# Interleaving the first two layer-norm tiles by halves, a shorter root chain, unread products on TensorE, and a convolution branch set back behind its first loads

## The chip, the cores and the metric

One core of one Trainium2 chip. The metric is the device time of one execution in microseconds (us), the median over several executions. "Before" is the kernel without the change, "after" the one with it.

## The reference

A layer norm of `x` feeds two branches whose outputs are added to `x`, and the kernel computes this forward pass together with all gradients for a given `grad_out`. Cut to what matters:

```python
def _fwd_reference(q, k, v, shift_k, ssm_k, ssm_D, x_unused, W_gate, W_up, W_down):
    xn = layernorm(q)                                   # (1, 2048, 1024), bf16
    # branch A: k shifted with 4 taps, times v, long convolution with ssm_k, times xn
    k_shift = sum(k_pad[:, t:t + S] * shift_k[:, 3 - t] for t in range(4))
    kv = k_shift * v
    y = irfft(rfft(kv) * rfft(ssm_k)) + kv * ssm_D
    a = xn * y
    # branch B: gated MLP, F = 3584
    b = (relu(xn @ W_gate) * (xn @ W_up)) @ W_down
    return q + a + b
# outputs: the sum, and its vector-Jacobian product with grad_out for q, k, v,
# shift_k, ssm_k, ssm_D, W_gate, W_up, W_down
```

## The kernel before

The big matrix products of the MLP keep TensorE busy nearly all the time. The convolution branch A is woven between them: both are Python generators that yield an estimate in nanoseconds of the TensorE work just emitted, and a loop takes the next step of branch A whenever the MLP has used up what the branch's last step asked for. So the numbers behind `yield` in the branch decide between which products its steps stand. A scheduler then fixes the order of instructions on each engine at build time, by a model of the machine and by priorities: copies and multiplications of branch A have a `late` priority and go where the model thinks VectorE or ScalarE idle.

The layer norm, one chunk of row tiles after the other (chunks of 1, 1, 2, 2, 2, 4, 4 tiles):

```python
    def layer_norm(self, xn_d, jpool, jtag, spool):
        ...
        for i, n in enumerate(self.LN_CHUNKS):
            ...
            for j in range(n):                                     # row sums on ScalarE
                total = nc.scalar.activation(out=jk[:], in_=xt[:, j, :], func=ACT.Copy, accum_out=sm[:, 0, j:j + 1])
            mean = V.tensor_scalar(out=b(0), in0=f(0), scalar1=1.0 / D, scalar2=None, op0=ALU.mult)
            V.tensor_copy(out=f(1), in_=b(0))
            for j in range(n):                                     # subtract on VectorE, squares on ScalarE
                V.tensor_scalar(out=xt[:, j, :], in0=xt[:, j, :], scalar1=sm[:, 1, j:j + 1], ..., op0=ALU.subtract)
                self.ln_act = nc.scalar.activation(out=jk[:], in_=xt[:, j, :], func=ACT.Square, accum_out=sm[:, 2, j:j + 1])
            ...                                                    # variance, eps, cast: three small operations
            self.ln_act = nc.scalar.activation(out=f(4), in_=f(3), func=ACT.Sqrt)
            V.reciprocal(out=f(5), in_=f(4))
            ...                                                    # five small operations: one Newton step
            self.ln_dve = V.reciprocal(out=self.rstd[:, st0:st0 + n], in_=f(10))
            for j in range(n):                                     # scale, store xn
                V.tensor_scalar(out=xt[:, j, :], in0=xt[:, j, :], scalar1=self.rstd[:, st:st + 1], ..., op0=ALU.mult)
                ...
            yield
```

(Some allocations of tiles and calls that set priorities are left out in these excerpts without a mark.) The MLP's first pass ("flip" transposes a tile of xn on TensorE, and VectorE copies it out of PSUM):

```python
                def gate_up(sp):
                    flip(sp + 2)
                    for s in (sp, sp + 1):
                        ps = self.ps_tile("ps_g")
                        self.gemm8(ps, xT[s], wg)
                        nc.scalar.activation(out=ru[s][:, 0, :], in_=ps[:], func=ACT.Relu)
                        yield 1730
                    for s in (sp, sp + 1):
                        ps = self.ps_tile("ps_u")
                        self.gemm8(ps, xT[s], wu)
                        nc.vector.scalar_tensor_tensor(out=ru[s][:, 1, :], in0=ru[s][:, 0, :], ..., in1=ps[:], ...)
                        ...                                        # ht = product of both, stored by SP
                        yield 1730
                if ahead:                                          # the first block only
                    flip(2)
                    next(ln)
                    yield from gate_up(0)
                    ...
```

The start of branch A, the transposes of its filter (`hn`, 16 of them into one PSUM tile `pst`), and the driver:

```python
    def h_tile(self, st):
        pst = self.ps.tile([P, 16, P], BF16, name="pst", tag="aps")     # pool "aps": two buffers
        for r in range(16):
            self.nc.tensor.transpose(pst[:, r, :], hv[:, r, :], self.identA[:])
        self.vcopy(hT[:, 0:16, :], pst[:])                              # VectorE, late priority

    def steps(self):
        ...
        nx = self.loads_1(0)
        self.loads_2(nx)
        self.pin = False
        hT = self.h_tile(nx)
        for gi in range(self.NG):                                       # eight channel groups
            yield 2000
            yield from self.fwd1_filter(hT, st["sD"], 2000)
            ...
            self.taps(st, ksh, kp, [(3, 0), (2, 1), (1, 2), (0, 3)])    # seven 128x2048 operations on VectorE
            self.tt(kvt[:, 0:16, :], ksh[:], vt[:], ALU.mult)           # and an eighth
            ...
            hT = self.h_tile(nx)                                        # for the next group
            yield 2000
            yield from self.inv_b_chan(Ch, ghn, 2000)                   # products RB x flp, two "aps" tiles
            ...

A_START = 55_000
    ...
    a_steps, left = a.steps(), A_START
    for pace, phase in mlp():
        for ns in phase:
            left -= ns * pace
            while a_steps is not None and left <= 0:
                d = next(a_steps, None)
                ...
                left += d
```

Of the kernel before, what the change touches and what calls it, by code (L numbers as in the profile page):

```python
# [11 lines left out]
BF16 = mybir.dt.bfloat16  # L12
F32 = mybir.dt.float32
I32 = mybir.dt.int32
ALU = mybir.AluOpType
ACT = mybir.ActivationFunctionType
AX = mybir.AxisListType
P = 128
# [24 lines left out]
class ABranch:  # L43
# [381 lines left out]
    def steps(self):  # L425


        self.shift_rows()
        self.pin = True
        nx = self.loads_1(0)  # L430
        self.loads_2(nx)
        self.pin = False
        hT = self.h_tile(nx)
        for gi in range(self.NG):
            st, nx = nx, None
            cg, kp, vt, gt = st["cg"], st["kp"], st["vt"], st["gt"]
            yield 2000
            yield from self.fwd1_filter(hT, st["sD"], 2000)
            Hf = self.flipped
            if gi == 0:  # L440
                self.gate_grad(st)
            ksh = self.lng.tile([P, 16, P], BF16, name="ksh")
            self.taps(st, ksh, kp, [(3, 0), (2, 1), (1, 2), (0, 3)])
            kvt = self.ttile("kvt")
            self.tt(kvt[:, 0:16, :], ksh[:], vt[:], ALU.mult)
            yield from self.fwd1(gt, 2000)
            Gf = self.flipped
            H = self.form("H")
            yield from self.fwd2(Hf, H, 1700)
            if gi + 1 < self.NG:  # L450
                nx = self.loads_1(gi + 1)
            yield from self.fwd1(kvt, 1800)
            Kf = self.flipped
            G = self.form("G")
            yield from self.fwd2(Gf, G, 1700)
            if nx is not None:
                self.gate_grad(nx)
            GKV = self.cmul(H, G, True, "GKV")
            yield 2000
            K = self.form("K")  # L460
            yield from self.fwd2(Kf, K, 1700)
            Y = self.cmul(H, K, False, "Y")
            yield 12000
            yield from self.inv_a(GKV, 1800)
            Cg = self.flipped
            yield 5000
            yield from self.inv_a(Y, 1800)
            Cy = self.flipped
            GH = self.cmul(K, G, True, "GH")
            yield 2000  # L470
            gkv = self.ttile("gkv")
            yield from self.inv_b(Cg, gkv, 2000)
            gks = self.gradients(st, gkv, ksh)
            yield 6000
            yt = self.ttile("yt")
            yield from self.inv_b(Cy, yt, 2000)
            self.store_time(self.y_d, cg, yt)
            yield from self.grad_taps(gi, gks, kp, 1800)
            self.grad_k(st, gks)
            if nx is not None:  # L480
                self.loads_2(nx)
            yield from self.inv_a(GH, 1800)
            Ch = self.flipped
            yield 3000
            if nx is not None:
                hT = self.h_tile(nx)
            yield 2000
            ghn = self.ttile("ghn")
            yield from self.inv_b_chan(Ch, ghn, 2000)
            ghf = ghn[:, 0:16, :].rearrange("p r c -> p (r c)")  # L490
            self.vcopy(self.gD_all[:, gi:gi + 1], ghf[:, 0:1])
            self.store(self.out_gh[cg, :], ghf)
            yield 6000
        self.small_outputs()
# [35 lines left out]
class LnMlp:  # L530
# [52 lines left out]
    def layer_norm(self, xn_d, jpool, jtag, spool):  # L583

        nc, D, V = self.nc, self.D, self.nc.vector

        st0 = 0
        for i, n in enumerate(self.LN_CHUNKS):
            xt = self.ln_x[i]
            self.pri.now()  # L590
            sm = spool.tile([P, 12, 4], F32, name="ln_s")
            smb = spool.tile([P, 4, 4], BF16, name="ln_b")
            f = lambda i: sm[:, i, 0:n]
            b = lambda i: smb[:, i, 0:n]
            for j in range(n):
                jk = jpool.tile([P, D], BF16, name="ln_j", tag=jtag)
                total = nc.scalar.activation(out=jk[:], in_=xt[:, j, :], func=ACT.Copy, accum_out=sm[:, 0, j:j + 1])  # L597
                if i >= 3 and j == 0:
                    self.tc.keep_in_program_order(total)
            mean = V.tensor_scalar(out=b(0), in0=f(0), scalar1=1.0 / D, scalar2=None, op0=ALU.mult)  # L600
            if i == 2:
                self.tc.keep_in_program_order(mean)
            V.tensor_copy(out=f(1), in_=b(0))
            for j in range(n):
                V.tensor_scalar(out=xt[:, j, :], in0=xt[:, j, :], scalar1=sm[:, 1, j:j + 1], scalar2=None,
                                op0=ALU.subtract)
                jk = jpool.tile([P, D], BF16, name="ln_j", tag=jtag)
                self.ln_act = nc.scalar.activation(out=jk[:], in_=xt[:, j, :], func=ACT.Square, accum_out=sm[:, 2, j:j + 1])
            V.tensor_scalar(out=b(1), in0=f(2), scalar1=1.0 / D, scalar2=None, op0=ALU.mult)
            V.tensor_scalar(out=b(2), in0=b(1), scalar1=LN_EPS, scalar2=None, op0=ALU.add)  # L610
            V.tensor_copy(out=f(3), in_=b(2))
            self.ln_act = nc.scalar.activation(out=f(4), in_=f(3), func=ACT.Sqrt)
            V.reciprocal(out=f(5), in_=f(4))
            V.tensor_tensor(out=f(6), in0=f(5), in1=f(5), op=ALU.mult)
            V.tensor_tensor(out=f(7), in0=f(6), in1=f(3), op=ALU.mult)
            V.tensor_scalar(out=f(8), in0=f(7), scalar1=-0.5, scalar2=1.5, op0=ALU.mult, op1=ALU.add)
            V.tensor_tensor(out=f(9), in0=f(5), in1=f(8), op=ALU.mult)
            V.tensor_tensor(out=b(3), in0=f(3), in1=f(9), op=ALU.mult)
            V.tensor_copy(out=f(10), in_=b(3))
            self.ln_dve = V.reciprocal(out=self.rstd[:, st0:st0 + n], in_=f(10))  # L620
            self.pri.now()
            for j in range(n):
                st = st0 + j
                V.tensor_scalar(out=xt[:, j, :], in0=xt[:, j, :], scalar1=self.rstd[:, st:st + 1], scalar2=None,
                                op0=ALU.mult)
                nc.gpsimd.dma_start(out=xn_d[st * P:(st + 1) * P, :], in_=xt[:, j, :])
                self.xn.append(xt[:, j, :])
            st0 += n
            yield
# [34 lines left out]
    def flip_xn(self, st):  # L664
# [4 lines left out]
        self.nc.vector.tensor_copy(out=xT[:], in_=pst[:].rearrange("p a b -> p (a b)"))  # L669
        return xT  # L670

    def hidden(self, first, goT, load, ln, tables, Wg, Wu, Wd, g, xn_d, h_d, ug_d):

        nc, HS = self.nc, self.ST // 2
        for half in range(2):
# [4 lines left out]
            for fb in range(self.FB):  # L680
# [10 lines left out]
                        xT.append(self.flip_xn(len(xT)))  # L691

                def gate_up(sp):
                    flip(sp + 2)
                    for s in (sp, sp + 1):
                        ru[s] = self.e2_tile("ru")
                        ps = self.ps_tile("ps_g")
                        self.gemm8(ps, xT[s], wg)
                        nc.scalar.activation(out=ru[s][:, 0, :], in_=ps[:], func=ACT.Relu)
                        yield 1730  # L700
                        self.pri.now()
# [3 lines that stand above are left out]
                        ht = self.e1_tile("ht")  # L705
                        nc.vector.scalar_tensor_tensor(out=ru[s][:, 1, :], in0=ru[s][:, 0, :], scalar=0.0, in1=ps[:],  # L706
                                                       op0=ALU.is_gt, op1=ALU.mult)
                        nc.vector.tensor_tensor(out=ht[:], in0=ru[s][:, 0, :], in1=ru[s][:, 1, :], op=ALU.mult)
                        stored = nc.sync.dma_start(out=h_d[(s0 + s) * P:(s0 + s + 1) * P, cols], in_=ht[:])
                        self.stored = stored  # L710
                        yield 1730
                        self.pri.now()

                def grad(sp):
                    for s in (sp, sp + 1):
# [9 lines left out]
                        yield 1730  # L725
                        self.pri.now()

                if ahead:
                    flip(2)
                    next(ln)  # L730
                    yield from gate_up(0)
                    next(ln)
                    yield from gate_up(2)
                    next(ln)
                for sp in range(0, HS, 2):
                    self.pri.now()
                    while len(gT) < min(sp + (6 if ahead else 2), HS):
# [4 lines left out]
                    if ahead and sp + 4 < HS:  # L742
                        with self.tc.issue_after(self.stored.ins):
                            load(5 + sp // 2)
                        yield from gate_up(sp + 4)
                        next(ln)
                    if ahead and sp == 0:
                        with self.tc.issue_after(self.stored.ins):
                            first = self.weights(Wg, Wu, Wd, fb + 1)
# [293 lines left out]
```

## Time and profile before

| | before |
|---|---|
| median of the first runs | 1954.47 us (1954.44 to 1956.24, 3 runs) |
| span of the profiled execution | 1957.4 us (its device time, 1959.14, is above those of the timed runs) |
| span of a second profile of the same program, taken later | 1954.3 us (device time 1956.03) |
| TensorE (PE) busy | 98% of the span |
| mean granted TensorE clock | 0.995 (first), 0.996 (second) |
| half-rate stretches of the clock on record (first profile) | from 93.2 us (6.8 us long), 127.3, 400.4 and 704.1 us (3.4 each) |

How to read the lines: "PE pst L293 <- DMA hn: 4.5, 1, 4.5" in the list of waits says that PE waited 4.5 us in total, once, for a load. A line of the timeline gives the start, the length, the engine, the source line, the operation with output, input and shape, the count, and in brackets how long the engine had been idle and what released it. The line numbers of the two kernels differ: L643 of before is L663 of after (the products), L667 is L687 (flips), L706 is L734 (eviction of the up product). `ru` is the tile into which the gate and up products are evicted; `ug_d` and `h_d` are its stores and those of `ht`. The small products of branch A have the operands `RH`, `R`, `FW`, `IA` and `RB`; `flp` is one of the branch's tiles flipped on VectorE, and `B` and `H` are copies out of PSUM made by ScalarE.

### The profile page before, as it was taken

The numbers are of one execution on the slowest core, as the hardware profiler recorded it, in microseconds if no ns is written. First come the engines' busy times: TensorE is split into PE (matmuls) and PEld (weight loads), VectorE is DVE, ScalarE is ACT, GpSimd is POOL, SyncE is SP. The second block draws the span as 40 slices with busy tenths as digits, with TensorE's granted clock in tenths as the row PEclk, the third lists the DMA queues.
The fourth block names the chain that finished last, engine by engine and source line by source line (L and its number), as shares of the span: only waits on it lengthen the run. The fifth ranks groups of instructions, "written<-read, shape, count | busy, mean of one in ns | idle before, by whom it ended". The sixth has DMA issues, their size and how long they took to land.

```text
span 1957.4 us, 36111 instructions
## 1 busy us (share of the span) xinstructions
PE 1915.1 (98%) x15502; PEld 882.0 (45%) x15502; DVE 914.1 (47%) x1374; ACT 616.8 (32%) x852; POOL 14.7 (1%) x37
## 2 busy tenths in 40 slices
PE   7899999999999999999999999999999999999998
PEld 3434444444444444444444444444444444444443
DVE  6677677577678557355255435300222222222222
ACT  6544354444444425444344354311000000000000
POOL 1000000000000000000000000000000000000000
PEclk9999999999999999999999999999999999999999
DMA  9975766984674774462763542691999954545441
GB/s 255 237 157 163 178 179 174 207 202 136 168 193 130 202 213 136 113 185 78 224 158 119 127 135 85 159 324 39 239 255 235 210 135 121 123 120 124 123 121 38
DMA packets 615970, 319.08 MB, mean 163 GB/s; under 512 B 450937, under 2 KB 585089, under 8 KB 615809
## 3 DMA queue, kind: packets, MB, share of 16 engines
q1 hardware_dynamic: 605312, 295.79, 60.2%
q10 hardware_dynamic: 9216, 16.78, 2.8%
q0 software_dynamic: 1280, 4.20, 0.8%
q8 instruction: 121, 1.98, 0.4%
q14 instruction: 41, 0.33, 0.1%
HBM read 141.56 MB, written 95.44 MB: 121 GB/s over the span
## 4 chain that ended last, share of the span: by engine, by line
PE 90%; DVE 4%; DMA 3%; issue 2%; ACT 1%; SPq 0%; POOL 0%; DVEq 0%; ACTq 0%; POOLq 0%
PE ps_w L774 20%; PE ps_x L908 19%; PE ps_o L874 10%; PE ps_g L643 9%; PE ps_u L643 9%; PE ps_d L774 8%; PE ps_h L643 8%; PE ps L66 6%; DMA ln_x<-in_A_q_dram 1%; PE ps_d L794 1%; DVE flp L304 1%; ACT ln_j L597 1%; DMA kp<-in_A_k_dram 1%; DVE gk L74 0%; DVE ru L706 0%
## 5 line engine op out<-in xcount | busy, mean ns | idle before, releaser
L774 PE MATMUL ps_w<-ugs,xn_nat 128*128 128x512 bf16 x1792 | 399.4, 379 | 2.1 <-DMA xn_nat<-xn_d 1.3
L643 PEld LDWEIGHTS <-xnT 128*128 128x128 bf16 x1792 | 172.2, 99 | 218.3 <-issue 19.6
L774 PEld LDWEIGHTS <-xn_nat 128*128 128x128 bf16 x1792 | 170.3, 98 | 208.6 <-issue 5.9
L643 PE MATMUL ps_u<-wu,xnT 128*128 128x512 bf16 x896 | 209.4, 384 | 4.7 <-DMA wu<-in_B_W_up_dram 4.1
L643 PE MATMUL ps_g<-wg,xnT 128*128 128x512 bf16 x896 | 209.0, 383 | 2.2 <-DVE xnT L669 2.2
L643 PE MATMUL ps_h<-wdT,goT 128*128 128x512 bf16 x896 | 206.7, 379 | 0.6 <-DMA wdT<-in_B_W_down_dram 0.6
L921 ACT ACTIVATE w<-xn,m 128x512 f32<-128x512 bf16 x32 | 24.3, 806 | 559.5 <-issue 317.2
L908 PE MATMUL ps_x<-wgT,ggT 128*128 128x512 bf16 x896 | 198.6, 379 | 0.0
L908 PE MATMUL ps_x<-wuT,guT 128*128 128x512 bf16 x896 | 198.6, 379 | 0.0
L874 PE MATMUL ps_o<-wd,hT 128*128 128x512 bf16 x896 | 193.6, 379 | 0.0
L774 PE MATMUL ps_d<-g_nat,hs 128*128 128x512 bf16 x832 | 187.4, 379 | 0.0
L304 DVE STREAM_TRANSPOSE flp<-C 128x1024 f32<-128x1024 f32 x48 | 90.4, 1934 | 102.8 <-ACT C L70 102.8
L829 ACT CAST wi<-ps_w 128x512 bf16<-128x512 f32 x112 | 65.6, 587 | 222.4 <-PE ps_w L774 207.9
L908 PEld LDWEIGHTS <-ggT 128*128 128x128 bf16 x896 | 87.7, 98 | 105.7
L908 PEld LDWEIGHTS <-guT 128*128 128x128 bf16 x896 | 87.7, 98 | 105.7
L874 PEld LDWEIGHTS <-hT 128*128 128x128 bf16 x896 | 87.7, 98 | 105.7
L643 PEld LDWEIGHTS <-goT 128*128 128x128 bf16 x896 | 85.1, 98 | 103.5 <-issue 4.5
L304 DVE STREAM_TRANSPOSE flp<-B 128x1024 f32<-128x1024 f32 x48 | 90.4, 1940 | 83.3 <-ACT B L70 83.2
L910 DVE CUSTOM_DVE_ANT_0 gx<-ps_x,gy 128x512 f32<-128x512 f32 x32 | 22.1, 691 | 216.5 <-PE ps_x L908 216.5
L774 PEld LDWEIGHTS <-hs 128*128 128x128 bf16 x832 | 78.5, 98 | 95.5 <-issue 4.3
L721 ACT CAST gh<-ps_h 128x512 bf16<-128x512 f32 x112 | 65.2, 585 | 165.7 <-PE ps_h L643 153.7
L867 DVE TENSOR_TENSOR ya<-ya,xe 128x1024 bf16<-128x1024 bf16 x16 | 11.1, 692 | 226.9 <-DMA xe<-xn_d 226.9
(165 smaller groups left out, 1541.6 us busy)
## 6 DMA issues: line engine op xcount, KB each, us to landing
ug_d<-ru SPq DMA_DIRECT2D x112, 256.0 KB, 3.5
ugs<-ug_d SPq DMA_DIRECT2D x112, 256.0 KB, 4.6
wg<-in_B_W_gate_dram SPq DMA_DIRECT2D x56, 256.0 KB, 4.2
wu<-in_B_W_up_dram SPq DMA_DIRECT2D x56, 256.0 KB, 3.4
h_d<-ht SPq DMA_DIRECT2D x112, 128.0 KB, 2.4
hs<-h_d SPq DMA_DIRECT2D x56, 256.0 KB, 4.7
out_dram<-wi SPq DMA_DIRECT2D x56, 256.0 KB, 3.1
gt<-in_grad_out_dram SPq DMA_DIRECT2D x32, 256.0 KB, 3.4
```

The costliest lines, as they stand in the source:

```text
L66: self.nc.tensor.matmul(out, lhsT=lhsT, rhs=rhs, start=start, stop=stop)
L304: self.nc.vector.transpose(out=df[:, c0:c0 + 32, :], in_=sf[:, c0:c0 + 32, :])
L597: total = nc.scalar.activation(out=jk[:], in_=xt[:, j, :], func=ACT.Copy, accum_out=sm[:, 0, j:j + 1])
L643: self.nc.tensor.matmul(ps[:], lhsT=xT[:, kt * P:(kt + 1) * P], rhs=w(kt), start=(kt == 0), stop=(kt == self.DT - 1))
L721: nc.scalar.copy(out=gh[:], in_=ps[:])
L774: self.nc.tensor.matmul(ps[:], lhsT=lhsT(st), rhs=rhs(st), start=(st == 0), stop=(st == self.ST - 1))
L794: nc.tensor.matmul(ps[i][:], lhsT=hs(st)[:, j * P:(j + 1) * P], rhs=gn[st][:, ob * 512:ob * 512 + 512], start=(st == 0), stop=(st == self. ...
L829: nc.scalar.copy(out=wo[:, d, :], in_=ps[:])
L874: nc.tensor.matmul(ps[:], lhsT=hT[:, kt, :], rhs=self.wd[:, kt, oc], start=(kt == 0), stop=(kt == self.FT - 1))
L908: nc.tensor.matmul(ps[:], lhsT=T[:, kt, :], rhs=W[:, kt, oc], start=(i == 0), stop=(i == n - 1))
L910: V.tensor_tensor_reduce(out=gx[:, oc], in0=ps[:], in1=gy[:, oc], scale=1.0, scalar=0.0, op0=ALU.add, op1=ALU.add, accum_out=m[:, ob:ob + 1])
L921: nc.scalar.activation(out=w[:, oc], in_=xn[:, oc], func=ACT.Identity, scale=m[:, 5:6], bias=m[:, 4:5])
```

## The change

Its intent is to start TensorE's work earlier: split the first tile's row sums between ScalarE and VectorE, let tile 0 be flipped and multiplied while tile 1 is still normed, cut five operations of the root chain to two, and run 28 products of zeros that nobody reads while TensorE would wait, so that its clock is up when the read ones come. A `yield 8000` stands behind the branch's first loads: these are issued where they were, and all later work of branch A comes 8000 ns (of the estimates behind `yield`) later among the MLP's products. The diff, cut:

```diff
         self.pin = False
+        yield 8000
         hT = self.h_tile(nx)
@@ layer_norm
+            cut = D // 2 if i == 0 else D
+            def row_sums(j, k, func):
+                self.ln_act = nc.scalar.activation(out=jk[:, 0:cut], in_=xt[:, j, 0:cut], func=func, accum_out=sm[:, k, j:j + 1])
+                if cut < D:
+                    if func is ACT.Square:
+                        V.tensor_tensor_reduce(out=jk[:, cut:D], in0=xt[:, j, cut:D], in1=xt[:, j, cut:D], ...)
+                    else:
+                        V.tensor_reduce(out=sm[:, k + 6, 0:1], in_=xt[:, j, cut:D], axis=AX.X, op=ALU.add)
...
-            V.tensor_scalar(out=b(1), in0=f(2), scalar1=1.0 / D, scalar2=None, op0=ALU.mult)
+            yield
+            var = average(2, b(1))
+            if i == 1:
+                self.tc.keep_in_program_order(var)
...
-            V.reciprocal(out=f(5), in_=f(4))
-            V.tensor_tensor(out=f(6), in0=f(5), in1=f(5), op=ALU.mult)
-            V.tensor_tensor(out=f(7), in0=f(6), in1=f(3), op=ALU.mult)
-            V.tensor_scalar(out=f(8), in0=f(7), scalar1=-0.5, scalar2=1.5, op0=ALU.mult, op1=ALU.add)
-            V.tensor_tensor(out=f(9), in0=f(5), in1=f(8), op=ALU.mult)
-            V.tensor_tensor(out=b(3), in0=f(3), in1=f(9), op=ALU.mult)
+            V.reciprocal(out=f(6), in_=f(4))
+            V.scalar_tensor_tensor(out=f(5), in0=f(3), scalar=0.5, in1=f(6), op0=ALU.mult, op1=ALU.mult)
+            V.scalar_tensor_tensor(out=b(3), in0=f(4), scalar=0.5, in1=f(5), op0=ALU.mult, op1=ALU.add)
@@ unread products
+    def warm(self, n):
+        z = self.e1_tile("warm")
+        self.nc.gpsimd.memset(z[:], 0.0)
+        ps = self.ps_tile("ps_warm")
+        for _ in range(n):
+            self.nc.tensor.matmul(ps[:], lhsT=z[:, 0:P], rhs=z[:], start=True, stop=True)
@@ hidden
                 def gate_up(sp):
-                    flip(sp + 2)
                     for s in (sp, sp + 1):
+                        flip(s + 1 if ahead and sp == 0 else sp + 2)
...
+                def chunk():
+                    next(ln)
+                    next(ln)
                 if ahead:
-                    flip(2)
+                    self.warm(28)
+                    chunk()
                     next(ln)
+                    flip(1)
+                    next(ln)
+                    chunk()
                     yield from gate_up(0)
```

## The prediction

> **What bounds the kernel now.** I read the busy times of the page first, then who TensorE (PE) waited for in the first 130 us, the timeline of PE at those waits, and the stretches with their granted clock.
>
> ```profile
> PE 1915.1 (98%) x15502; PEld 882.0 (45%) x15502; DVE 914.1 (47%) x1374; ACT 616.8 (32%) x852; POOL 14.7 (1%) x37
> ```
>
> PE is busy in 1915.1 of 1957.4 us, so all a schedule can win is the other 42 us and whatever PE does slowly. From about 130 us on the list of PE's waits holds only some 10 us, and the last 8 us are the tail after the last product (ends 1949.4). The rest is early:
>
> ```profile
> PE pst_x L667 <- DVE ln_b L609: 10.4, 1, 10.4
> PE pst L293 <- DMA hn<-in_A_ssm_k_dram: 4.5, 1, 4.5
> PE ps_u L643 <- DMA wu<-in_B_W_up_dram: 4.1, 1, 4.1
> PE ps_g L643 <- DVE xnT L669: 2.2, 2, 1.1
> PE pst_x L667 <- DVE ln_x L624: 2.1, 1, 2.1
> ```
>
> The first line is the start: no flip before the first layer norm is done. The second and third are loads that the in-order DMA queue of SP issued late. The timeline of PE at the start:
>
> ```profile
> 10.37 1.03 PE L667 MATMUL pst_x<-ident,ln_x 128*128 128x128 bf16 x8 [10.37 <-DVE ln_b L609]
> 13.45 1.03 PE L667 MATMUL pst_x<-ident,ln_x 128*128 128x128 bf16 x8 [2.05 <-DVE ln_x L624]
> 14.28 5.50 PE L643 MATMUL ps_g<-wg,xnT 128*128 128x512 bf16 x16
> 19.61 3.62 PE L643 MATMUL ps_u<-wu,xnT 128*128 128x512 bf16 x16
> ```
>
> Sixteen products of the same shape take 5.50 us at 14.28 and 3.62 us at 19.61: PE is slow at first. Behind the wait for hn the same is seen, and there the clock is on record:
>
> ```profile
> 94.24 1.92 PE L293 MATMUL pst<-ident,hn 128*128 128x128 bf16 x16 [4.49 <-DMA hn<-in_A_ssm_k_dram]
> 95.95 3.19 PE L643 MATMUL ps_u<-wu,xnT 128*128 128x512 bf16 x7
> 98.94 1.55 PE L66 MATMUL ps<-hT,RH 128*128 128x512 bf16 x4
> ```
> ```profile
> 15.00:16.00 1.00, 1.00 (x4) 0.32 (x3) 0.93 (x5) 0.00 (x0) 0.00 (x0) 1.00 0.19 64
> 97.00:98.00 1.00, 1.00 (x4) 0.29 (x2) 0.42 (x1) 0.00 (x0) 0.00 (x0) 0.50 1.35 164
> 128.00:129.00 1.00, 1.00 (x4) 0.39 (x3) 0.97 (x2) 0.00 (x0) 0.00 (x0) 0.50 0.67 146
> ```
>
> The column before the DMA share is the granted clock: 0.50 at 97 and 128 us, just after the two long waits. At 15 us it says 1.00, yet PE does the same four products in that microsecond; the record of the clock begins with its rise at 18.1 us, so the first slow stretch must be read from the pace.
>
> **What the Trainium skill says.** "TensorE: Matmul & The Clock Gate", section Part 1: The HAM clock gate: the clock starts at half rate, rises after a busy window of about 3.4 us that runs free of the kernel, and falls again after an idle one; 512 columns take 426.7 ns cold, 215.7 warm. The trace agrees: weight loads 0.427 us apart until 18.1, then 16 products in 3.45 net. It adds that 2.3 us of waiting can be enough[...] (half rate at 400 us, after such a wait). "VectorE: DVE Perf Modes", section The perf-mode tier table: tensor_reduce runs at one element per cycle only; this trace has none. The same page, section The TRN2 errata: small operations pay a fixed cost; here a 128x1 VectorE operation takes 0.16 us and the next of a chain starts 0.19 to 0.20 later.
>
> **The change, part by part.**
>
> *Tile 0's norm.* Before: row sum on ScalarE from 3.59 (1.06, plus 0.19 to read the accumulator), usable at 4.77; subtraction 5.15 to 5.63; squares to 6.82; var, eps and cast to 7.38; square root only at 7.76, since tile 1's row sum stands before it; then reciprocal, five small operations, cast, reciprocal, done at 9.78; scaling ends 10.31. After: ScalarE sums 512 columns (estimate 0.53 + 0.19, half of 1.04 plus a fixed part), VectorE the others (estimate 0.65 from 512 cycles). Mean at 4.35, subtraction to 5.2, half squares to 5.98, cast to 6.55. The order of ScalarE still puts tile 1's full row sum (5.87 to 6.83) ahead of the root, so root 6.92 to 7.11. Then reciprocal and two fused operations for reciprocal and five, in all three fewer (0.6 us), but tile 1's mean, cast and subtraction (0.9) lie between. Scaling ends near 9.2: 1.1 us gained.
>
> *Order of flips.* Before, VectorE's queue holds the copy of xnT 0 behind tile 1's whole root chain (flip ends 11.4, copy starts 13.31). After, the copy stands directly behind tile 0's scaling.
>
> *28 unread products.* They start when GpSimd has zeroed their tile, about 1.5 us. They run cold for 3.4 to 6.8 us (where the window lies is chance): 8 to 16 products at 0.427, the rest at 0.216, so they end between 9.2 and 10.9. PE was idle there, but they can hold the flip back by up to 1.7 us. The flip is then warm (16 take 1.06, so 0.53), copy 0.68 + 0.05: first product 10.6 to 12.2 against 14.28.
>
> *Tile 1.* VectorE takes var 1 up only after that copy: three small operations, root, five more, scaling, about 2.45 us: 13.05 to 14.6. Flip 0.53; but tile 2's mean and two subtractions (1.3) stand before the copy, so tile 1's products start 15.1 to 16.6, while tile 0's eight ended 12.3 to 13.9. A new wait of some 2.5 us, partly filled by the flip. Eight gate and sixteen up products at 0.216: end 20.3 to 21.8 against 23.0. Net gain of the start 1.2 to 2.7, less up to 1.6 if the new wait makes the clock fall: I take 1.5.
>
> *The 8000 in the convolution branch.* It moves the transposes of hn behind eight more up and eight down-gradient products (16 x 0.216 = 3.5 us), and the DMA order puts hn one ug store (0.6 us) earlier. hn took 89.19 to 94.24. PE came at 89.75; now it comes 1.5 earlier plus 3.5 later, 91.75; hn's issue moves with the tables, 1.5 + 0.6 earlier, to 87.1, and lands 92.15. Wait 0.4 instead of 4.5. Then no cold stretch: 16 transposes lose 0.6 there, seven up products 1.5, four of RH 0.9, together 3.0. Gain 7.
>
> *The later wu wait.* Before, wu was issued at 122.09 because the ug stores ahead of it waited for two multiplications on VectorE with a 1.9 us flip between (ends 118.98 + 1.93, 120.77 + 0.67). Now the two stand together behind the filter's flips. Counted from the first transposes of hn: PE has 72 products of 512 (15.5) and 5.3 us of branch work before it needs wu, 20.8; flips end 16.1, multiplications 17.5, wu is issued 18.2 and lands 4.4 later, 22.6. Wait 1.8 instead of 4.05, and the 1.7 us lost cold behind it probably too: 3.5 gained.
>
> Sum 1.5 + 7 + 3.5 = 12. The shorter root chains of later chunks hide behind PE.
>
> **Rivals.** (1) The unread products cost what they win: they end late, or zeros don't raise the clock. For: 28 cold ones would last 12 us, to 13.5, and the start would win nothing; total then about 1945. Against: the page speaks of activity, not of values. (2) The waits move instead of going: hn's 4.5 us come back at the filter's flips or at wu, as VectorE and the SP queue stay in order. For: wu is still in the same place behind the stores, and my margin is 2 us. Then only 4 to 6 are won: 1949. (3) Most is luck of interleaving: shifting the branch changes every later meeting of it with the products; the waits after 130 us (10 us, two with a cold stretch of about 1.6) may be won or doubled, 1936 or 1950. (4) The start decides all and the rest follows unchanged: 1.5 to 4 us, 1951.
>
> **Range and chances.** 1954.5 - 12 = 1942.5. Spread: start +-1.5, hn +-2, wu +-3.5, later interleaving +-5; in quadrature 6.6, a little wider upwards: 1935 to 1951. Two per cent are 39 us; PE's own work alone forbids a win that size, and nothing added costs as much.
>
> **What would show it.** The copy of xnT 0 directly behind the scaling near 9.2; first read product at 0.216 pace between 10.6 and 12.2; a wait of about 2 us before tile 1's; end of the first sixteen up products 20 to 22. Hn's wait under 1 us and clock 1.00 from 85 to 105 us; wu's wait under 2.5. Wrong if the unread products still run after 11 us, if the clock falls again before 30 us, or if the sum of PE's waits after 130 us differs by over 5 us.

## The result, and the profile after

After: 1958.3 us median (1955.94 to 1959.82, 4 runs); before, in the same rounds, 1954.45 (1952.49 to 1956.24, 4 runs). The ratio is 1.0019 with a 95% interval of 1.0001 to 1.0036. A ratio here is the mean time of one kernel's fast runs over that of the other's of the same rounds, so not quite the ratio of the medians. Predicted were 1942.5 with a range up to 1951: the change was to win 12 us and lost about 4.

The busy times of the page, and the head of the list of PE's waits, both of after:

```profile
PE 1919.8 (98%) x15530; PEld 884.3 (45%) x15530; DVE 913.0 (47%) x1356; ACT 617.0 (32%) x852; POOL 15.4 (1%) x38
```
```profile
PE ps L66 <- DVE hT L78: 9.7, 4, 2.9
PE ps_g L663 <- DVE ru L734: 3.9, 2, 3.2
PE ps_g L663 <- DVE xnT L689: 3.4, 3, 1.3
...
PE ps L66 <- ACT B L70: 1.6, 2, 1.1
PE ps_warm L698 <- POOL warm L695: 1.5, 1, 1.5
```

The three early waits of before (10.4 us for the first norm, 4.5 for hn, 4.1 for wu) are gone from the list. In their place PE waits more for hT (9.7 us; 6.1 before), and for `ru`, an eviction on VectorE, which was not in the list before.

**The start** went as it was meant to; tile 0's scaling on VectorE ended at 9.21 us (near 9.2 foreseen). The timeline of PE in after:

```profile
1.48 9.14 PE L698 MATMUL ps_warm<-warm 128*128 128x512 bf16 x28 [1.48 <-POOL warm L695]
10.46 0.61 PE L687 MATMUL pst_x<-ident,ln_x 128*128 128x128 bf16 x8
11.85 1.90 PE L663 MATMUL ps_g<-wg,xnT 128*128 128x512 bf16 x8 [0.79 <-DVE ln_b L615]
14.03 0.62 PE L687 MATMUL pst_x<-ident,ln_x 128*128 128x128 bf16 x8 [0.28 <-DVE ln_x L644]
15.83 1.90 PE L663 MATMUL ps_g<-wg,xnT 128*128 128x512 bf16 x8 [1.18 <-DVE xnT L689]
17.57 3.62 PE L663 MATMUL ps_u<-wu,xnT 128*128 128x512 bf16 x16
21.02 1.06 PE L687 MATMUL pst_x<-ident,ln_x 128*128 128x128 bf16 x16
```

Eight gate products take 1.90 us at 11.85: the clock is up. The flips of tiles 2 and 3 begin at 21.02; before they began at 23.06.

**The wait for hn** is gone, and with it the half rate. PE's timeline of after, and the row of the stretch 97 to 98 us (busy time and count of each engine, then the granted clock, the DMA share and GB/s), where before's clock was 0.50:

```profile
90.55 1.18 PE L293 MATMUL pst<-ident,hn 128*128 128x128 bf16 x16
...
93.29 0.59 PE L66 MATMUL ps<-hT,RH 128*128 128x512 bf16 x2
```
```profile
97.00:98.00 1.00, 1.00 (x6) 0.44 (x5) 1.00 (x1) 0.63 (x2) 0.00 (x0) 1.00 1.35 173
```

**The wait for wu** is gone too, but two others stand in its place. PE's timeline at wu of before, then that of after, then VectorE's (DVE) of after:

```profile
126.52 5.60 PE L643 MATMUL ps_u<-wu,xnT 128*128 128x512 bf16 x16 [4.05 <-DMA wu<-in_B_W_up_dram]
```
```profile
111.22 0.42 PE L66 MATMUL ps<-flp,FW 64*32 64x128 bf16 x32 [1.05 <-ACT B L70]
...
114.53 4.66 PE L663 MATMUL ps_u<-wu,xnT 128*128 128x512 bf16 x16
119.03 3.62 PE L663 MATMUL ps_h<-wdT,goT 128*128 128x512 bf16 x16
125.88 5.30 PE L663 MATMUL ps_g<-wg,xnT 128*128 128x512 bf16 x16 [3.23 <-DVE ru L734]
```
```profile
115.70 1.21 DVE L74 TENSOR_TENSOR ksh<-kp,skb 128x2048 bf16<-128x2048 bf16 x1
...
124.00 1.22 DVE L74 TENSOR_TENSOR kvt<-ksh,vt 128x2048 bf16<-128x2048 bf16 x1
125.14 0.68 DVE L734 SCALAR_TENSOR_TENSOR ru<-ru,ps_u 128x512 bf16<-128x512 bf16 x1
```

At 114.53 the up products start without waiting for wu. But the 128 flp products ahead of them, which in before stood in two groups of 64 with 24 big products between, now stand together, and each quarter of them waits for a copy by ScalarE of an earlier tile (1.05, 0.50, 0.50 and 0.41 us); the clock then falls to half (16 products in 4.66 us instead of 3.62). And the up products' results stay in PSUM until VectorE evicts them at 125.14, behind 9.4 us of tap products; PE waits 3.23 us for that buffer and the clock falls again (5.30 us). In before the same taps ran on VectorE from 121.36 to 130.8; the wait for wu (122.47 to 126.52) lay beside 4.05 of these 9.4 us, and no wait for `ru` followed.

**Late in the kernel** the waits for hT grew. One place, the same in both programs: the 16 transposes of hn and then the two halves of RB x flp. PE and then VectorE of after, followed by PE and VectorE of a second profile of before, taken later:

```profile
546.00 0.63 PE L66 MATMUL ps<-RB,flp 128*128 128x64 bf16 x16
...
551.24 0.63 PE L66 MATMUL ps<-RB,flp 128*128 128x64 bf16 x16 [2.88 <-DVE hT L78]
```
```profile
548.23 1.22 DVE L74 TENSOR_TENSOR ksh<-ksh,tap 128x2048 bf16<-128x2048 bf16 x1
...
549.97 1.22 DVE L78 COPY hT<-pst 128x2048 bf16<-128x2048 bf16 x1
```
```profile
544.24 0.63 PE L66 MATMUL ps<-RB,flp 128*128 128x64 bf16 x16
...
546.51 0.63 PE L66 MATMUL ps<-RB,flp 128*128 128x64 bf16 x16
```
```profile
545.24 1.22 DVE L78 COPY hT<-pst 128x2048 bf16<-128x2048 bf16 x1
```

The second half needs the PSUM buffer that the transposes hold until VectorE has copied them out. In after the first half comes one step of eight products sooner behind the transposes (2.73 us after their start at 543.27, against 4.47 after 539.77 in before), and the copy 1.2 us later (6.70 us against 5.47). So PE waits 2.88 us here; before, nothing.

**Where the time goes, in one table.** I took from each trace the time from each product's start to the next one's, less the median of that for products of the same shape, and added these up: the time that TensorE has lost up to a point, in us. The 28 unread products count as lost where they exist (28 x 0.2157 = 6.04). The four traces hold all their products.

| lost up to (us) | 21 | 80 | 100 | 140 | 400 | 1300 |
|---|---|---|---|---|---|---|
| before, second profile | 15.3 | 18.1 | 24.4 | 32.5 | 46.1 | 91.4 |
| after | 13.3 | 16.0 | 16.0 | 26.3 | 38.8 | 91.5 |
| after without the 8000 | 12.9 | 18.4 | 20.1 | 28.0 | 41.1 | 86.0 |
| before with the 8000 | 15.4 | 19.1 | 20.0 | 30.1 | 43.1 | 92.9 |

After against before: 2.0 won at the start, 6.2 between 80 and 100 us (hn), 2.1 lost between 100 and 140, 1.1 won up to 400, 7.4 lost up to 1300. The sum is nothing, as the spans say (1954.1 and 1954.3). The medians differ by about 4 us, since after's profile fell on its fastest run and before's second profile on the slowest of its five; so some 2 to 4 us of the loss are in runs that were not traced. One trace's figure for the late part is itself uncertain by one or two us: after 140 us after has lost 6.3 more than the second profile of before, but only some 5 more than the first.

The 6.3 are not all waits. The lists of waits after 130 us sum to 14.2 us in after and to 10.0 and 10.7 in the two profiles of before; much of the rest are products at half rate: the clock's record has stretches of 3.4 us at half rate from 717.4 and 847.1 us in after, each at a wait for hT, and from 701.2 alone in the second profile of before.

### The profile page after: what moved, and what is told of

Same layout as the page of the kernel before. It is cut to its first block, busy times and chain, and to the rows that moved or that the text cites. A ratio compares the mean times of both kernels' runs of the same rounds, so it can differ in the third digit from the quotient of the medians.

```text
span 1954.1 us, 36167 instructions
## 1 busy us (share of the span) xinstructions
PE 1919.8 (98%) x15530; PEld 884.3 (45%) x15530; DVE 913.0 (47%) x1356; ACT 617.0 (32%) x852; POOL 15.4 (1%) x38
## 4 chain that ended last, share of the span: by engine, by line
PE 88%; DVE 5%; DMA 3%; issue 2%; SPq 1%; ACT 0%; POOL 0%; DVEq 0%; POOLq 0%; ACTq 0%
PE ps_w L810 19%; PE ps_x L944 19%; PE ps_o L910 10%; PE ps_g L663 9%; PE ps_h L663 8%; PE ps_u L663 8%; PE ps_d L810 8%; PE ps L66 6%; DVE tap L74 1%; DMA out_dram<-gv 1%; DVE flp L304 1%; DVE gk L74 1%; DVE ksh L74 1%; DMA kp<-in_A_k_dram 1%; DMA xn_nat<-xn_d 1%
## 5 line engine op out<-in xcount | busy, mean ns | idle before, releaser
L734 DVE SCALAR_TENSOR_TENSOR ru<-ru,ps_u 128x512 bf16<-128x512 bf16 x112 | 76.4, 682 | 83.2 <-PE ps_u L663 36.1
```

## The experiments

Theory 1: the start wins what it should, and the 8000 loses more than it wins, because the branch's new places among the products bring new waits. Rival: the unread products or the norm cost something; or the loss after 130 us is noise of single traces. Each run was timed five times, unless said otherwise, and the ratio is against before on the same chip and rounds.

### The spread: before, unchanged

> The kernel before, unchanged, as a yardstick of how far two copies of one program differ in time and in the waits of TensorE. Every theory: ratio 1.000 within 0.001. If the later waits are fixed by the program, the trace shows the same waits at 398 and 701 us (2.7 and 2.8 us); if they are chance of the run, they differ by a few us in sum.

Median 1955.68, ratio 1.0003 (0.999 to 1.0017). A difference of 0.0013 and more can be read from five runs, about 2.5 us. The late waits are the program's: the trace has those for hT again (2.39 and 2.46 us, ending at 399.2 and 700.3). What follows a wait is not. The wait at 400 us in the first profile of before, then in the second:

```profile
400.46 1.03 PE L66 MATMUL ps<-RB,flp 128*128 128x64 bf16 x16 [2.29 <-DVE hT L78]
```
```profile
399.16 0.64 PE L66 MATMUL ps<-RB,flp 128*128 128x64 bf16 x16 [2.39 <-DVE hT L78]
```

The first was followed by 3.4 us at half rate, the second, a longer wait of the same program, by none.

### The start and the 8000, each alone

The first takes `yield 8000` out of after, the second puts it into before:

```diff
         self.pin = False
-        yield 8000
         hT = self.h_tile(nx)
```

> The change without the 8000 in the convolution branch; TensorE's order is then that of before but for the first 40 read products. Theory 1 (the shift wins at hn and wu and gives it back in the later meetings of branch and products; the start itself wins about 2 us): about 2 us faster than before, ratio 0.998 to 0.9995, hn's wait of 4 to 5 us back, later waits as in before. Theory 2 (the start costs later what it wins, by the unread products or the earlier traffic): ratio 1.000 to 1.003. Theory 3 (the change won 10 us and the measured difference is run-to-run noise): ratio near 0.999 too, told apart by the next run.

```diff
         self.pin = False
+        yield 8000
         hT = self.h_tile(nx)
```

> The kernel before with only the 8000 in the branch; TensorE's order is then that of the change but for the first 40 read products. Theory 1: hn's wait gone, yet slower than before by 3 to 7 us (ratio 1.0015 to 1.0035), with waits of 3 us before the last step of the branch at about 550, 716 and 847 us. Theory 2: faster than before by 5 to 9 us, ratio 0.9955 to 0.9975.

Without the 8000: 1950.6, ratio 0.9985 (0.9973 to 0.9998). The 8000 alone: 1960.55, ratio 1.0029 (1.0016 to 1.0042). With both (after) 1.0019. So the start is worth -2.9 us (0.0015 x 1954), the 8000 +5.7 (0.0029 x 1954), and the sum, +2.8, is near after's +3.7. The programs make this a clean square: on TensorE the first differs from before in only 32 places of 15502 (the start), and the second from after in 16. The two waits that the 8000 brings are in the second's list of waits, without any change at the start:

```profile
PE ps L66 <- DVE hT L78: 8.9, 4, 3.0
PE ps_g L644 <- DVE ru L707: 4.0, 2, 3.3
```

In after without the 8000 the wait for hT is 6.0 as before, and that for `ru` is not in the list. Theory 1 holds in the times, and the table above shows it by stages. One forecast of it missed: without the 8000 the wait for hn was 1.4 us, not 4 to 5. With the new start alone the load is issued 2.8 us sooner than before (86.43 against 89.19), while PE comes for it only 0.4 sooner (89.3 against 89.75), having lost a wait of 2.51 us at 48.3 with half rate behind it. So by 100 us each part alone has won about the same (4.3 and 4.4), and both together 8.4.

### No unread products

```diff
                 if ahead:
-                    self.warm(28)
                     chunk()
```

> The change without the 28 unread products; the order of the rest is the same. Theory 1: the first flip comes at 9.3 instead of 10.46, but eight to sixteen read products run at half rate (1.7 to 3.4 us), so the first sixteen up products end about 0.5 to 2 us later than 21.0, and the time is 0 to 2 us longer than the change's: 1.0019 to 1.003 over before. Theory 2: 2 to 4 us faster than the change, at or under the time of before.

Median 1958.9, ratio 1.0022 (1.0008 to 1.0036), against after's 1.0019. TensorE's order is after's. PE's timeline:

```profile
11.05 3.59 PE L663 MATMUL ps_g<-wg,xnT 128*128 128x512 bf16 x8 [0.79 <-DVE ln_b L615]
...
21.26 1.06 PE L687 MATMUL pst_x<-ident,ln_x 128*128 128x128 bf16 x16
```

The first gate products start 0.80 us sooner, since nothing holds the flip back (it is at 9.23 instead of 10.46), but take 3.59 us instead of 1.90. At 21 us the unread products are worth 0.24 us in this pair of traces, and the times do not tell the two kernels apart.

### No halves, and the old root chain (one run each)

```diff
-            cut = D // 2 if i == 0 else D
+            cut = D
```

> The change with tile 0's row sums whole on ScalarE; read from the trace, not from the time. If the unread products (end 10.46 in the change) and not the norm set the first flip, the flip stays within 0.5 us of 10.5 though tile 0's scaling ends later than 9.2 (by 0.5 to 0.9), and the first sixteen up products end at 21.0 to 21.6. If the norm sets it, the flip moves by the full 0.5 to 0.9.

The other puts the old root chain back into after:

```diff
-            V.reciprocal(out=f(6), in_=f(4))
-            V.scalar_tensor_tensor(...)                               # two fused operations
+            V.reciprocal(out=f(5), in_=f(4))
+            V.tensor_tensor(out=f(6), in0=f(5), in1=f(5), op=ALU.mult)
+            ...                                                       # and the other four, as in before
```

> The change with the root chain of before (three operations more per chunk); read from the trace. Tile 0's scaling ends 0.5 to 0.6 later (9.8), tile 1's too, so the second flip moves from 14.03 to about 14.6, and the first sixteen up products end 0.6 later, about 21.6.

Each was run once, without timing rounds, in an unknown state: 1961.28 and 1964.25 us, which tells nothing at a spread of several us. TensorE's order in both is after's exactly. What the traces tell is the start: the flips of tiles 2 and 3 begin at 20.91 without halves and at 21.19 with the old chain (after: 21.02). So neither piece is seen at the end of the start, and the forecasts missed: the first flip without halves came at 9.99, set by the norm and not by the unread products (these ended at 9.47 in that run), and the old chain was to cost 0.6 us by 21 and cost 0.2. What is left of the change there is the order of flips, copies and norms; that this is what wins the 2 us is argued by elimination, and neither this order alone nor the change without both pieces was tried.

### Is it hT's copy? On ScalarE instead, with and without the 8000

```diff
-        self.vcopy(hT[:, 0:16, :], pst[:])
+        self.act(hT[:, 0:16, :], pst[:])
```

> The change with the copy of hT (128x2048, 1.22 us on VectorE) moved to ScalarE, all else the same; TensorE's order is the same in all but 30 of 15502 products. Theory 1a (what the shift gives back after 300 us are the waits of 3 us before the second half of the branch's last step, which needs the PSUM buffer that VectorE frees only after its backlog of tap products): TensorE's waits put down to hT (9.7 us) fall under 2 us, two stretches at half clock (near 716 and 847 us) go, total 8 to 12 us shorter than the change: ratio to before 0.9955 to 0.998. Rival (the wait is for the flips on VectorE or for ScalarE's own copies, hT is only the last to signal): waits of the same length stay, ratio 1.001 to 1.003.

The same edit in after without the 8000:

```diff
         self.pin = False
-        yield 8000
...
+        self.act(hT[:, 0:16, :], pst[:])
```

> The start of the change, no shift, hT's copy on ScalarE. Theory 1a: the 6 us of waits at hT and one stretch at half clock (1.7) go as well: 5 to 8 us less than the no-shift run's 1950.6, ratio 0.994 to 0.9965. If the shift's only loss was at hT, this is slower than e5 by some 5 us (hn and wu waits are back); if the loss at 105 to 130 us counts too, the two come out within 3 us.

In after: 1949.19 (6 runs), ratio 0.9974 (0.9961 to 0.9987), which is 0.0045 or 9 us below after's ratio. Its wait:

```profile
PE ps L66 <- ACT hT L70: 3.8, 2, 2.7
```

9.7 us in four waits became 3.8 in two; the one that ended at 551.24 us, shown above, is gone, and so are the half-rate stretches at 717 and 847 us. A wait of 2.75 us that ends at 715.3 is still there, with no half rate behind it in this trace. Without the 8000, however, the same edit gave 0.9992 (0.998 to 1.0004) against 0.9985 without it: nothing won (5 to 8 us were forecast), and PE waits 6.1 us for ScalarE's copy where it had waited 6.0 for VectorE's. So the copy behind VectorE's other work is a cost of the 8000's places, and moving it isn't good in itself.

### Other delays

```diff
-        yield 8000
+        yield 4000
```

> The change with 4000 in place of 8000. Theory 1 (each shift deals the meetings of branch and products anew, and no size is better on principle): hn's wait 0 to 3 us, other waits in other places, ratio 0.998 to 1.004, not between the runs with 0 and 8000 for any reason. Rival (a longer delay of the branch costs in proportion): ratio half-way, 1.000 within 0.001.

```diff
-        yield 8000
+        yield 16000
```

> The change with 16000 in place of 8000. Theory 1: ratio anywhere in 0.997 to 1.005, waits of hT's kind 5 to 13 us in sum. Rival (cost in proportion to the delay): 1.005 to 1.007.

4000: 1952.99, ratio 0.999 (0.9978 to 1.0002). 16000: 1952.01, ratio 0.9986 (0.9974 to 0.9999). With 0 (0.9985) and 8000 (1.0019) this is no trend with the delay: 8000 is a bad place among four. That speaks for chance of interleaving, and against delay as such.

### The same delay, started 8000 sooner

```diff
-A_START = 55_000
+A_START = 47_000
```

> The change with the branch begun 8000 earlier (47000 in place of 55000), so that the 8000 only puts its loads earlier and every later product of the branch is where it was without the shift (TensorE's order differs from the no-shift run's in 64 of 15502 products). Theory 1: the early gain without the new deal: hn's wait under 1 us with no stretch at half clock behind it, later waits as in the no-shift run, ratio 0.9965 to 0.9985. Rival (hn's load is bound by the tables on ScalarE, not by its place in the queue): hn's wait grows by up to 6 us, ratio 0.999 to 1.002.

This issues the branch's loads sooner but leaves its transposes among nearly the products of before (64 places differ from after without the 8000). 1949.65, ratio 0.9967 (0.9955 to 0.998): faster than before by 0.3% and than after by 0.5%. PE's timeline:

```profile
85.47 1.22 PE L293 MATMUL pst<-ident,hn 128*128 128x128 bf16 x16
...
118.30 0.38 PE L663 MATMUL ps_u<-wu,xnT 128*128 128x512 bf16 x1 [2.10 <-DMA wu<-in_B_W_up_dram]
```

hn is there when wanted; the wait for wu is back in full (4.4 us in four pieces), and the waits for hT are 6.5 us, as in before. So hn's gain is real and can be had without the 8000's losses. Against the run without the 8000 (0.9985, 0.9973 to 0.9998) the intervals overlap, so how much of the time it wins is not shown. In this run the clock fell once more at 15.6 us, at the two waits of tile 1, and the flips of tiles 2 and 3 began at 22.60 instead of 21.02. The clock's record shows the same, from 14.9 to 16.1 us, in 6 of the 15 traces with the new start: there most of the start's 2 us is lost again.

### One tap instead of four

```diff
-            self.taps(st, ksh, kp, [(3, 0), (2, 1), (1, 2), (0, 3)])
+            self.taps(st, ksh, kp, [(3, 0), (2, 1), (1, 2), (0, 3)][:1 if gi == 0 else 4])
```

> The change with three of the four taps of the first channel group left out (outputs of that group wrong on purpose), so VectorE's series of tap products after 115 us lasts 2.5 us instead of 9.4. Theory 1b (the 3.6 us that TensorE loses at 122 us are the wait for a PSUM buffer behind that series, and the stretch at half clock after it is its echo): both go, 4 to 6 us less than the change, ratio 0.999 to 1.000. Rival (TensorE waits there for something else): the wait stays, ratio 1.0015 to 1.0025.

Wrong results on purpose (relative error 0.31). 1960.57, ratio 1.0026 (1.0012 to 1.004). It missed: the wait of 3.2 us for `ru` is gone, but the scheduler, seeing kvt ready sooner, put its products right behind the flp ones, and PE waits there:

```profile
122.37 1.04 PE L66 MATMUL ps<-kvt,R 64*128 64x512 bf16 x4 [3.59 <-DVE kvt L74]
```

The clock is at half rate for 13.7 us from 117.3. (The traced execution, 1966.51, was the slowest of the five; the others took 1959.64 to 1960.82.) Since TensorE's order changed, it did not tell what the taps cost in the order of after.

### The taps behind the eviction

For the first channel group alone the taps are emitted after the filter's second stage:

```diff
-            self.taps(...); kvt = ...; self.tt(kvt, ksh, vt)          # before fwd1(gt)
+            if gi == 0: self.taps(...); ...                           # just before fwd1(kvt)
             yield from self.fwd1(kvt, 1800)
```

> The changed kernel with the taps of the first channel group (and their product with v) emitted after the filter's second stage instead of before it. On VectorE one tap product then stands ahead of the evictions of ps_u instead of eight operations (9.4 us); on TensorE the order differs from the changed kernel's only at 84 places, all between about 119 and 165 us. Theory (the wait at 126 us and its half-clock stretch are caused by the taps in front of the eviction): the 3.2 us wait on ru disappears and with it the stretch at half rate (5.30 us for 16 products instead of 3.6, then partly 1.89): 4 to 5 us less time lost by 140 us, median 1953.5 to 1954.5 if nothing of it is given back. Rival (the loss only moves, as in the run with one tap): a wait for kvt of 2 us or more takes its place, and the time lost at 140 us differs from the changed kernel's by under 2 us; median 1956.5 to 1959.

TensorE's order differs from after's at 84 places, all between 119 and 165 us. 1960.5, ratio 1.0028 (1.0015 to 1.0041). PE's timeline:

```profile
124.53 3.62 PE L669 MATMUL ps_g<-wg,xnT 128*128 128x512 bf16 x16
...
142.86 0.60 PE L66 MATMUL ps<-kvt,R 64*128 64x512 bf16 x4 [0.48 <-DVE kvt L74]
...
147.60 0.42 PE L66 MATMUL ps<-flp,FW 64*32 64x128 bf16 x32 [0.45 <-ACT B L70]
```

The gate products at 124.53 wait for nothing and run at full rate, so the taps were the cause of the wait at 125.88 and of the half rate behind it. But the branch's products that come later for it now stand close together, and PE waits for ScalarE's copies there (0.45, 0.50 and 0.50), for `ru` (0.71) and for wdT (0.48). The theory's local part is right and so is the rival's outcome: nothing is left of it in the time. Its trace can be set beside the one without halves, which has the order of after and lacks as many products (15291 of 15530 recorded): lost from 120 to 140 us are 0.5 against 4.3, from 140 to 180 us 7.1 against 2.9.

### The taps behind the eviction, and hT's copy on ScalarE

```diff
+            if gi == 0: self.taps(...); ...                           # as in the run before
...
-        self.vcopy(hT[:, 0:16, :], pst[:])
+        self.act(hT[:, 0:16, :], pst[:])
```

> First group's taps later, and hT's copy on ScalarE: both of the new waits taken away at once. If the two are independent terms of the same loss, the times add: the run with hT on ScalarE alone was 0.9974 of the kernel before, less 4 to 5 us (0.0023): ratio 0.995, median near 1945, which is near what was predicted for the change. If interleaving gives one back, ratio 0.997 or more.

1952.85, ratio 0.9991 (0.9979 to 1.0003), no better than hT's copy alone (0.9974; the intervals just overlap). Both traces lack the same number of products (15291 of 15530 recorded), so their sums of lost time can be set side by side: from 120 to 140 us 1.2 against 4.0, so 2.8 won by moving the taps; from 140 to 180 us 7.2 against 2.9, so all of it given back. The two gains do not add. But against the run with the taps alone (1.0028) hT's copy on ScalarE wins 0.0037, about 7 us: a second pair with the 8000 in which it wins.

### The taps of all groups

```diff
-            self.taps(...); kvt = ...; self.tt(kvt, ksh, vt)          # for every group, before fwd1(gt)
...
+            self.taps(...); kvt = ...; self.tt(kvt, ksh, vt)          # for every group, just before fwd1(kvt)
             yield from self.fwd1(kvt, 1800)
```

> As the run before, but for all channel groups. TensorE's order differs from the changed kernel's at 116 places. If the late waits for hT's copy on VectorE come from the taps alone that stand before it, they shrink too (9.7 us of waits on hT to under 6) and the time is 2 to 4 us under that of the run with the first group's taps moved. If it is any VectorE work, the waits stay at 8 to 11 us and the time is the same within 2 us.

1959.37, ratio 1.0022 (1.001 to 1.0034), the same as with the first group's within the interval; PE waits 10.7 us for hT. That does not clear the taps, for on VectorE they hardly moved: in the trace the ten operations ahead of hT's copy near 549 us are the same in the same order as in after, four of them tap operations, and before the copies near 715, 847 and 1130 us the taps stand as well. The scheduler put them there although they are emitted later. The run leaves open whether the taps in front of the copy cause the waits.

### The fastest version with hT's copy on ScalarE

```diff
-A_START = 55_000
+A_START = 47_000
...
-        self.vcopy(hT[:, 0:16, :], pst[:])
+        self.act(hT[:, 0:16, :], pst[:])
```

> The changed kernel with the branch started 8000 sooner (ratio 0.9967 before) and hT's copy on ScalarE. That kernel has 6.5 us of waits on hT's copy like the kernel before; moving the copy won nothing where the order was that of the kernel before (0.9992 against 0.9985). Expected by that: 0.996 to 0.998, no gain over the run without it. If the copy's engine counts in any order: 0.994.

1951.07 (6 runs), ratio 0.9977 (0.9965 to 0.9988): no gain over 0.9967, as expected from the pair without the 8000. So moving hT's copy won 9 and 7 us in the two pairs with the branch in after's late places, and nothing in the two with it in those of before.

## Why the prediction was wrong

**What bounds the kernel**: right. PE stayed 98% busy; what moved was only its waits and its clock.

**The start, 1.5 us**: right, 2.0 in the traces and 2.9 by the times of after without the 8000. The first read product came at 11.85 (10.6 to 12.2 foreseen), the sixteen up products ended at 21.0 (20.3 to 21.8), the unread ones at 10.6 (9.2 to 10.9). The reasons were half right: the unread products were worth 0.24 us, and neither the halves nor the short chain is seen at 21 us; rival 1 (they cost what they win) describes them well, but cost the total next to nothing. The risk that the clock falls behind tile 1's wait did not strike in after's trace, but did in 6 of the 15 with the new start.

**hn, 7 us**: right in sum, 6.2 against the second profile of before and 7.4 against the first. No wait, clock 1.00. The load was issued at 85.17, not at 87.1. But the 8000 alone does not win it: the start alone had cut the wait to 1.4 us, the 8000 alone to 0.7.

**wu, 3.5 us won**: this step failed; 2.1 us were lost between 100 and 140. The queue of SP was worked out well: wu was issued at 108.75, 18.2 us after hn's transposes (90.55), as the prediction says. Wrong was the path of PE: it was to need wu after 20.8 us and wait 1.8, but came only after 24.0 (at 114.53), held up by other waits, so none for wu was left. Not followed was what PE meets on this path with the new order: flp products without big products between them (2.5 us of waits for ScalarE's copies, and 1.0 at half rate), and behind wu the 9.4 us of taps on VectorE, 4.05 of which had lain beside the old wait, and which now stood ahead of an eviction (3.23 us, and 1.7 at half rate). This is rival 2, "the waits move instead of going", but at another place than it named. The run with the taps moved shows the taps as the cause of the wait for `ru`, and also that undoing it gives the time back by 180 us. That the flp products wait because nothing stands between them is read from the traces and was not tried.

**Later interleaving, 0 +-5**: this step failed most. It was named as a rival (3) and as a spread, but the centre was put at zero and the spread treated as independent of the rest. The traces show 6.3 us lost after 140 us (some 5 against the first profile of before), and the times ask for some more. The prediction's own sign, the sum of PE's waits after 130 us, moved by only 3.5 to 4.2, below its mark of 5: it did not count what half rate adds behind a wait. Shown: the 8000 alone costs 5.7 us with the old start; hT's copy on ScalarE takes 9 us from after and nothing from the version without the 8000; 4000 and 16000 don't have the loss. These are timed differences, so it isn't noise of single traces. It is this one set of places, and hT's PSUM buffer is the largest part of it that an experiment shows.

**Rival 4** (the start decides all, 1951) is what after without the 8000 does: 1950.6.

Summed again with what was measured: -2.0 (start), -6.2 (hn), +2.1 (100 to 140), +6.3 (after 140) is 0.2 in this pair of traces, against -12 predicted; the median says +4, and the rest is in runs without a trace. Open are those 2 to 4 us, and what in VectorE's queue holds hT's copy up.

## What to carry to other kernels

A wait during which other engines did work of their own is not free to remove: before counting it as won, list what ran beside it on VectorE and ScalarE and see which eviction or buffer that work will then stand in front of. In a woven schedule at 98% busy, a shift of one branch is a new draw of all later meetings: here 8000 cost 5.7 us, and none of the three delays was faster than none. Try several shifts, and put the early load ahead of its use (here by starting the branch sooner) instead of moving the use back. A wait of two or three us may or may not be followed by half rate, even in the same program, so take more than one profile. Single waits don't add: two that were each shown to be real, taken away together, won no more than one of them alone.

## What the Trainium skill lacked or had wrong

- "TensorE: Matmul & The Clock Gate", Part 1: The HAM clock gate. Its table gives one idle window of some 3.4 us as what brings the clock down. Here shorter idling was enough: 2.29 us at 398 us of before was followed by half rate from 400.4, and in the run started at 47000 the clock fell at waits of 1.30 and 1.18 us with eight transposes (0.62 us) between them. It is not certain to fall: 2.39 us at the same place in the second profile of before, and 1.48 and 1.18 us in the run with the old root chain, did not bring it down. The page does not say whether products of zeros count as activity for this gate: they do, as 28 of them took 9.14 us in after, where 28 at the 0.427 us apart of before's first products would take 12.0, and the clock's record rises at 7.4 us, when TensorE had run nothing else.
- "TensorE: Matmul & The Clock Gate", Part 4: PE-mode transpose. It measures 390 ns for one 128x128 bf16 transpose alone and about 275 in a kernel. One of hn's took 219 to 235 ns in after, but they overlap: a series of 16 took 1.06 us at full clock (66 ns each) and 1.92 at half, so their pace follows the clock. The page has no figure for a series.
- "VectorE: DVE Perf Modes", The perf-mode tier table. It has tensor_reduce at one element per cycle, but no duration for it: 128x512 bf16 took 0.69 us, against the 0.65 estimated. One size alone does not show the rate.
